# Linear attention and a gated MLP on one core: keys turned to token rows on the array's quarters, odd heads' values stored once, new loads and a new order

## The chip, the cores and the metric

The kernel runs on one core of one Trainium2 chip. The metric is device time in microseconds (us) of one execution. The engines of the core are named as the profile names them: PE (TensorE, matmuls; PEld is its weight load), DVE (VectorE), ACT (ScalarE), POOL (GpSimd) and SP (SyncE), which here only issues DMAs.

## The reference

```python
f = 1.0 / (1.0 + np.exp(-f_logit))                       # (4, 8, 768, 48) each: batch, head, token, dim
for t in range(S):
    state = f[:, :, t, :, None] * state + np.einsum('bhd,bhe->bhde', k[:, :, t], v[:, :, t])
    y[:, :, t] = np.einsum('bhd,bhde->bhe', q[:, :, t], state)
x = y.transpose(0, 2, 1, 3).reshape(B, S, 384)
h = np.maximum(x @ w_in, 0.0)                            # w_in 384 x 1024
u, v = h[..., :512], h[..., 512:]
v_n = (v - mean(v)) / np.sqrt(var(v) + 1e-06)
v_s = np.einsum('ts,bsd->btd', w_spatial, v_n) + b_spatial[None, :, None]
return (u * v_s) @ w_out                                 # w_out 512 x 384
```

The first half is gated linear attention with a forget gate per key dimension. The second half is an MLP in which one half of the hidden layer is mixed over tokens by `w_spatial` and gates the other half.

## The kernel before, in words

The whole kernel is one list of steps, `PLAN`, written out in the file. A step such as `K:4` calls `step_K(4)`, which issues its few instructions at once; every engine then works through its own instructions in that order, and semaphores hold an instruction back until its inputs are there. So the list sets each engine's queue, SP's queue of loads included.

The attention works on 24 chunks n of 128 tokens (4 batch rows of 6 chunks), all 8 heads together. Heads go in pairs: the even head of a pair lies on partitions 0 to 47, the odd one on 64 to 111, and four pairs j lie side by side. The steps of a chunk are:

- `LF`, `LK`, `LQ`: loads of the gate's logits, of keys and queries (tile `fkq`), and of values (`val`). From chunk 8 on `LF` brings logits, keys and queries together.
- `c`, `e`, `z`: the log of the gate and its running sum (chunks 0 to 7 by 8 matmuls with a triangle, L309; later ones by a DVE scan). `h`, `g`, `k`, `q`, `fm`: the decays (`F`), and keys and queries scaled by them.
- `X`: 16 matmuls of 48 by 64, keys against queries within 64 tokens (L359, tile `bp`); `m` masks them on DVE into `sc` (L362).
- `K`: four transposes of 112 by 128 that bring the keys to one token per partition (L341, tile `mm`); `w` copies them to `W` on ACT (L344).
- `kv`: 16 matmuls, keys by values, one sum per 64 tokens (L376, tile `bp`); `r0` and `r1` add them to the state on DVE (`sB`, `sA`).
- `YS`: 16 matmuls, scores by values (L402, `bp`). `Yq`: up to 16, queries by state (L415), added in the same place. `ys` copies the sum to `ysb` on ACT, `xt` transposes it in three pieces (L427), `xh` and `xl` split it into two parts for exact products.

The MLP's steps on PE are `V` (9 matmuls, the half that is normalised, L460), `U` (9, the other half, L545), `S` (18, the spatial mixing, L559) and `O` (12, the output, L590). `vr`, `bs`, `vn`, `vh`, `vl` and others around them normalise on DVE and ACT. `ca`, `ct`, `ch`, `cl` and `wh`, `wl` turn loaded weights into pairs of parts. One `S` needs the normalised rows `vnh`, `vnl` of all six chunks of a batch row.

PSUM is held as four tiles of one bank (`mm`) and two of two banks (`bp`). `take` and `done` hand them out in the order of the list: `X`, `kv` and `Yq`/`YS` each take a `bp` tile, while `K`, `z`, `xt`, `V`, `U`, `S` and `O` take an `mm` tile. A tile is free again when its readers are through.

PE can run as one array of 128 by 128 (here: `K`, `xt`, `V`, `U`, `S`, `O`), as two of 128 by 64 (`z`) or as four quarters of 64 by 64 (`X`, `kv`, `YS`, `Yq`), which work beside each other.

In the code that follows, `even`, `odd`, `low` and `high` are the partition slices 0:48, 64:112, 0:64 and 64:128. Each program line has the number that the profile gives it.

Of the kernel before, what the change touches and what calls it, by code (L numbers as in the profile page):

```python
# [19 lines left out]
T = 128  # L20
# [6 lines left out]
VW = HD + J * D  # L27
# [18 lines left out]
    LF:0 LK:0 constants W0 LF:1 c:0 LQ:1 e:0 LQ:0 z:0 LF:2 c:1 LV:0 e:1 h:0 z:1 g:0 q:0 LK:1 h:1 k:0 g:1 c:2 LW:0,0  # L46
    K:0 fm:0 e:2 fm:1 X:0 LO:1 m:0 ca:V,0 z:2 q:1 w:0 YS:0 k:1 wh:0,0 LK:2 kv:0 ct:V,0 K:1 LQ:2 w:1 ca:O,1 LV:1 r0:0
    ch:V,0 r1:0 Yq:0 ys:0 cl:V,0 X:1 LF:3 h:2 xt:0 LK:3 m:1 g:2 fm:2 q:2 xh:0 YS:1 LW:2,0 ca:V,1 k:2 kv:1 c:3 K:2
    LU:1 ct:V,1 e:3 w:2 z:3 wh:2,0 LQ:3 r0:1 ch:V,1 LB r1:1 Yq:1 cl:V,1 h:3 X:2 LF:4 g:3 LK:4 m:2 fm:3 ca:U,1 q:3
    YS:2 ys:1 LU:0 k:3 kv:2 c:4 xt:1 r0:2 e:4 K:3 xl:0 Yq:2 LQ:4 r1:2 w:3 V:0,0 ys:2 wl:0,0 LK:5 xh:1 wl:2,0 ca:U,0  # L50
    LF:5 xt:2 xl:1 LW:1,0 X:3 vr:0,0 ct:U,0 z:4 xh:2 W1 V:0,1 h:4 g:4 m:3 fm:4 ch:U,0 k:4 YS:3 wh:1,0 xl:2 kv:3
    vr:0,1 K:4 c:5 LQ:5 r0:3 V:0,2 r1:3 e:5 cl:U,0 w:4 q:4 Yq:3 vr:0,2 z:5 ct:O,1 LK:6 ys:3 X:4 h:5 LF:6 U:0,0,1 g:5
    fm:5 nm:0,0 ch:O,1 m:4 U:0,0,0 q:5 vc:0,2 c:6 vc:0,1 k:5 e:6 YS:4 wl:1,0 kv:4 sq:0,1 K:5 ct:U,1 LQ:6 z:6 sq:0,2
    w:5 xt:3 vc:0,0 r0:4 xh:3 r1:4 Yq:4 ch:U,1 xl:3 X:5 LF:7 h:6 cl:U,1 moe V:0,3 LK:7 ys:4 m:5 fm:6 g:6 sq:0,0 q:6
    xt:4 k:6 ur:0,0,1 YS:5 xh:4 na:0,0 kv:5 c:7 nb:0,0 K:6 xl:4 LQ:7 e:7 nc:0,0 U:0,0,2 r0:5 vh:0,0 r1:5 cl:O,1 Yq:5
    vh:0,2 X:6 LO:0 vl:0,0 ur:0,0,2 ys:5 z:7 m:6 vr:0,3 vl:0,2 w:6 YS:6 LF:8 bs:0,3 h:7 kv:6 g:7 xt:5 q:7 V:0,4
    vh:0,1 r0:6 fm:7 LQ:8 r1:6 xh:5 ca:O,0 k:7 Yq:6 xl:5 ur:0,0,0 X:7 LF:9 c:8 vr:0,4 V:0,5 m:7 ys:6 bs:0,4 e:8
# [722 lines left out]
```

## Time and profile before

| what | value |
|---|---|
| median of 3 runs | 370.69 us (369.97 to 371.74) |
| the profiled execution | 371.09 us, of which the span from first to last instruction is 368.9 us |
| PE busy | 349.8 us, 95% of the span |
| DVE, ACT, POOL busy | 219.5, 179.2, 49.7 us |
| mean granted PE clock | 0.974 |
| loaded and stored | 36.27 MB |

A busy PE is one with a matmul under way. Since PE is busy for nearly all of the span, the time is read as PE's work in order of time, plus what it waits for at the start, plus the end after its last matmul.

### The profile page before, as it was taken

The numbers are of one execution on the slowest core, as the hardware profiler recorded it, in microseconds if no ns is written. First come the engines' busy times: TensorE is split into PE (matmuls) and PEld (weight loads), VectorE is DVE, ScalarE is ACT, GpSimd is POOL, SyncE is SP. The second block draws the span as 40 slices with busy tenths as digits, with TensorE's granted clock in tenths as the row PEclk, the third lists the DMA queues.
The fourth block names the chain that finished last, engine by engine and source line by source line (L and its number), as shares of the span: only waits on it lengthen the run. The fifth ranks groups of instructions, "written<-read, shape, count | busy, mean of one in ns | idle before, by whom it ended". The sixth has DMA issues, their size and how long they took to land.

```text
span 368.9 us, 10624 instructions
## 1 busy us (share of the span) xinstructions
PE 349.8 (95%) x4674; PEld 321.0 (87%) x4674; DVE 219.5 (60%) x428; ACT 179.2 (49%) x351; POOL 49.7 (13%) x68
## 2 busy tenths in 40 slices
PE   4589999999999999999999999999999999999992
PEld 3478778889989989999999888999988989999992
DVE  2777788899888555774235898641558537123120
ACT  5774688773574355653135664522355335221121
POOL 3000000001211201012102221032200001122120
PEclk9955999999999999999999999999999999999998
DMA  8997146441554014440045421300171000100102
GB/s 277 351 314 247 49 120 230 121 137 44 151 153 120 0 35 130 123 126 2 0 128 157 140 77 32 118 25 1 34 226 36 2 24 21 44 0 2 43 21 73
DMA packets 13829, 36.27 MB, mean 98 GB/s; under 512 B 1488, under 2 KB 7120, under 8 KB 13776
## 3 DMA queue, kind: packets, MB, share of 16 engines
q1 hardware_dynamic: 13776, 35.53, 31.3%
q8 instruction: 38, 0.62, 0.7%
q14 instruction: 15, 0.12, 0.1%
HBM read 30.80 MB, written 4.72 MB: 96 GB/s over the span
## 4 chain that ended last, share of the span: by engine, by line
PE 86%; DMA 7%; DVE 3%; ACT 1%; SPq 1%; issue 0%; ACTq 0%; DVEq 0%
PE mm L559 28%; PE mm L590 13%; PE mm L460 13%; PE mm L545 13%; DMA fkq<-fkq 4%; PE bp L415 3%; PE bp L402 3%; PE bp L359 3%; DMA fkq<-fn 3%; PE bp L376 3%; PE mm L341 3%; PE mm L427 2%; PE mm L309 1%; DMA out<-osb 1%; DVE fkq L326 0%; SPq L280 0%
## 5 line engine op out<-in xcount | busy, mean ns | idle before, releaser
L575 POOL TENSOR_TENSOR uT<-gt,uT 128x384 f32<-128x384 f32 x32 | 37.7, 1177 | 177.1 <-DVE gt L568 106.9
L583 DVE TENSOR_TENSOR gl<-uT,gh 128x384 fp32r<-128x384 f32 x32 | 18.5, 579 | 40.0 <-ACT gh L579 34.3
L559 PE MATMUL mm<-w_sph,vnh 128*128 128x384 f32 x192 | 40.0, 343 | 0.0
L559 PE MATMUL mm<-w_spl,vnh 128*128 128x384 f32 x192 | 39.0, 338 | 0.0
L559 PE MATMUL mm<-w_sph,vnl 128*128 128x384 f32 x192 | 39.0, 338 | 0.0
L559 PEld LDWEIGHTS mm<-w_sph,vnl 128*128 128x128 f32 x192 | 34.2, 188 | 0.0
L559 PEld LDWEIGHTS mm<-w_spl,vnh 128*128 128x128 f32 x192 | 34.2, 188 | 0.0
L559 PEld LDWEIGHTS mm<-w_sph,vnh 128*128 128x128 f32 x192 | 33.5, 188 | 0.3
L550 ACT ACTIVATE uT<-mm 128x384 f32<-128x384 f32 x32 | 15.7, 490 | 36.7 <-PE mm L545 36.7
L568 DVE TENSOR_TENSOR gt<-mm,b_bc 128x384 f32<-128x384 f32 x32 | 17.7, 553 | 25.8 <-PE mm L559 25.6
L579 ACT CAST gh<-uT 128x384 fp32r<-128x384 f32 x32 | 16.4, 512 | 29.1 <-POOL uT L575 28.2
L336 POOL COPY ends<-F 112x4 f32<-112x4 f32 x24 | 10.1, 425 | 129.2 <-ACT F L315 129.2
L607 ACT COPY osb<-mm 128x384 f32<-128x384 f32 x24 | 11.5, 478 | 32.0 <-PE mm L590 27.0
L545 PE MATMUL mm<-xTh,w_inh 128*128 128x384 f32 x96 | 23.6, 354 | 0.0
L298 ACT ACTIVATE fkq<-fkq 112x512 f32<-112x512 f32 (+1 forms) x24 | 14.3, 596 | 17.4 <-DVE fkq L294 17.3
L460 PE MATMUL mm<-w_inh,xTh 128*128 128x512 f32 x72 | 22.6, 423 | 0.1
L474 ACT ACTIVATE vr<-mm 128x512 f32<-128x512 f32 x24 | 14.3, 596 | 16.7 <-PE mm L460 13.0
L362 DVE TENSOR_TENSOR sc<-bp,mask 128x512 f32<-128x512 f32 x24 | 16.5, 686 | 9.7 <-PE bp L359 9.6
L590 PE MATMUL mm<-w_outh,gh 128*128 128x384 f32 x96 | 22.2, 348 | 0.0
L545 PE MATMUL mm<-xTh,w_inl 128*128 128x384 f32 x96 | 22.1, 338 | 0.0
L545 PE MATMUL mm<-xTl,w_inh 128*128 128x384 f32 x96 | 22.0, 338 | 0.0
L304 DVE TENSOR_TENSOR_SCAN fkq<-runs,fkq 112x512 f32<-112x512 f32 x16 | 19.4, 1217 | 3.4 <-ACT fkq L299 3.3
(102 smaller groups left out, 728.7 us busy)
## 6 DMA issues: line engine op xcount, KB each, us to landing
fkq<-fkq SPq DMA_DIRECT2D x16, 672.0 KB, 4.8
val<-vv SPq DMA_DIRECT2D x24, 288.0 KB, 3.5
out<-osb SPq DMA_DIRECT2D x24, 192.0 KB, 2.2
fkq<-fkq SPq DMA_DIRECT2D x8, 448.0 KB, 4.1
words<-w_cv SPq DMA_DIRECT2D x4, 768.0 KB, 6.7
fkq<-fn SPq DMA_DIRECT2D x8, 192.0 KB, 4.0
late<-w_cv SPq DMA_DIRECT2D x2, 768.0 KB, 7.3
spat<-w_spT SPq DMA_DIRECT2D x3, 384.0 KB, 5.6
```

What stands on the lines that cost most here:

```text
L298: nc.scalar.activation(f, f, AF.Exp, scale=-1.0)
L304: return nc.vector.tensor_tensor_scan(f[0:DP], runs, f[0:DP], 0.0, op0=ALU.mult, op1=ALU.add)
L362: nc.vector.tensor_tensor(Ss[n % 2].rearrange("p (e j t) -> p e j t", e=2, t=C), bp.of(("X", n))[:, :, 0:J * C].rearrange("p e (j t) -> p ...
L460: nc.tensor.matmul(acc, xs[:, c, ut * P:(ut + 1) * P], ws[:, c, G:FF], start=i == 0, stop=i == 3 * KX - 1)
L545: nc.tensor.matmul(acc[:, 0:TH], ws[:, kx, cs], xs[:, kx, :], start=i == 0, stop=i == 3 * KX - 1)
L550: nc.scalar.activation(uTs.take((b, th, c)), mm.of(("u", b, th, c))[:, 0:TH], AF.Relu)
L559: nc.tensor.matmul(acc[:, 0:TH], vns.of((b, ks))[va][:, cs], w_sp_s[wb][:, ks, th * TH:(th + 1) * TH], start=i == 0, stop=i == 3 * KS - 1,)
L568: nc.vector.tensor_tensor(gts.take((b, th, c)), mm.of(("s", b, th, c))[:, 0:TH], b_bc[:, th * TH:(th + 1) * TH], op=ALU.add)
L575: nc.gpsimd.tensor_tensor(uT, gts.of((b, th, c)), uT, op=ALU.mult)
L579: nc.scalar.copy(gs.take((b, th, c), HU)[0], uTs.of((b, th, c)))
L583: nc.vector.tensor_tensor(lo, uTs.of((b, th, c)), hi.bitcast(F32), op=ALU.subtract)
L590: nc.tensor.matmul(acc[:, 0:DM], gs.of((b, th, c))[ga][:, ts], w_out_s[wb][:, c, :], start=c == cs[0] == 0 and ga == wb == 0, stop=c == cs ...
```

## The change

Four things change together.

1. `K` no longer makes four transposes of the whole array. It makes 16 small products against the identity, on the quarters, into the unused columns of the same two banks that hold the chunk's scores. Those that land on partitions 0 to 63 are transposes, those that land on 64 to 127 are ordinary matmuls. `w` then copies 384 columns instead of 448, and `K` takes no `mm` tile. The `bp` tile of the scores is held until both `m` and `w` are through.
2. `kv` writes into the free columns of the bank pair that `YS` has opened, so it follows `YS` and takes no `bp` tile of its own; that pair is held until both `ys` and `r1` are through. Its weights are 48 columns for every head, where the even heads' were 64.
3. Values of odd heads are stored once, with the two halves of the chunk exchanged, instead of twice: a `val` load is 128 x 384 instead of 128 x 576. `fkq` and `w_cv` are laid out in DRAM so that a partition's row comes in three, two or two pieces instead of one. There are four `fkq` tiles instead of three and three `val` tiles instead of two.
4. `PLAN` is a new order of the same 1,079 steps; `W0` and `W1`, which held one `mm` tile for a time and issued nothing, are gone. `LO:1`, `LW:0,0` and others move later, `LF:1` and `LF:3` earlier.

The core of the diff, with the first line of each list:

```diff
-    LF:0 LK:0 constants W0 LF:1 c:0 LQ:1 e:0 LQ:0 z:0 LF:2 c:1 LV:0 e:1 h:0 z:1 g:0 q:0 LK:1 h:1 k:0 g:1 c:2 LW:0,0
+    LF:0 constants LF:1 LQ:1 LK:0 c:0 e:0 LK:1 c:1 e:1 z:0 LV:0 z:1 h:0 g:0 q:0 LQ:0 h:1 k:0 LF:3 g:1 q:1 LV:1 X:0
...
-    ins = tiles(attn, "fkq", 3, [P, 3, J * T])
-    vals = tiles(attn, "val", 2, [P, VW])
+    ins = tiles(attn, "fkq", 4, [P, 3, J * T])
+    vals = tiles(attn, "val", 3, [P, HD])
...
-    Ws = tiles(attn, "W", 2, [P, J * DP])
+    Ws = tiles(attn, "W", 2, [P, 2, J * D])
...
-            nc.sync.dma_start(ins[n % 3][0:DP], fkq[b, u])
+            nc.sync.dma_start(ins[n % 4][0:DP], fkq[b, u].rearrange("i p n -> p i n"))
...
-    def step_K(n):
-        tr = mm.take(("kT", n))
-        for j in range(J):
-            nc.tensor.transpose(tr[:, j * DP:(j + 1) * DP], parts(n)[1][:, j * T:(j + 1) * T], ident[0:DP, 0:DP])
-
-    def step_w(n):
-        nc.scalar.copy(Ws[n % 2], mm.of(("kT", n))[:, 0:J * DP])
-        mm.done(("kT", n))
...
+    def quarters(j):
+        a, b = slice(j * T, j * T + C), slice(j * T + C, (j + 1) * T)
+        return (even, low, a), (odd, high, a), (even, high, b), (odd, low, b)
+
+    def scores(n):
+
+        if ("X", n) not in bp.held:
+            bp.take(("X", n), 2)
+        return bp.of(("X", n))
+
+    def step_K(n):
+        tr = scores(n)
+        for j in range(J):
+            cs = slice(J * C + j * D, J * C + (j + 1) * D)
+            for (e, dr), to, at in quarters(j):
+                k = parts(n)[1][dr, at]
+                if to is low:
+                    nc.tensor.transpose(tr[to, e, cs], k, ident[dr, dr])
+                else:
+                    nc.tensor.matmul(tr[to, e, cs], k, ident[dr, dr], start=True, stop=True)
+
+    def step_w(n):
+        nc.scalar.copy(Ws[n % 2], scores(n)[:, :, J * C:J * C + J * D])
+        bp.done(("X", n))
...
-        W, v, pp = Ws[n % 2], vals[n % 2], bp.take(("kv", n))
+
+        W, v, pp = Ws[n % 2], vals[n % 3], bp.of(("y", n))
...
-            for (e, dr), chunk, rows in ((even, 0, low), (odd, 1, high), (odd, 0, low), (even, 1, high)):
-                out, m = (low, slice(j * DP, j * DP + C)) if e == 0 else (dr, slice(j * DP + C, (j + 1) * DP))
+            for (e, dr), chunk, rows in ((even, 0, low), (odd, 0, high), (even, 1, high), (odd, 1, low)):
...
-                nc.tensor.matmul(pp[out, chunk, cs], W[rows, m], v[rows, hd], start=True, stop=True)
+                nc.tensor.matmul(pp[dr, chunk, J * D:][:, cs], W[rows, e, cs], v[rows, hd], start=False, stop=True, skip_group_check=True)
...
-        bp.done(("kv", n))
+        bp.done(("y", n))
...
-        s, v, y = Ss[n % 2], vals[n % 2], bp.take(("y", n))
+        s, v, y = Ss[n % 2], vals[n % 3], bp.take(("y", n), 2)
...
-        "fkq": np.stack([pairs(f_logit, 10.0), pairs(k, 0.0), pairs(q, 0.0)], axis=3),
+        "fkq": np.stack([pairs(f_logit, 10.0), pairs(k, 0.0), pairs(q, 0.0)], axis=2),
...
-        "vv": np.concatenate([vt, odd], axis=-1),
+        "vv": vt.reshape(B, NU, T, HD),
```

Where the new order bears on the time, the rows of the engines' queues stand as follows. The number behind a name is the buffer: `bp_132` and `bp_133` are the two bank pairs, `fkq_112`, `_113`, `_114` (and `_115`) the tiles of logits, keys and queries, `val_115` and so on the values.

SP's queue of loads from its start, before:

```order
L280 DMA fkq_112<-fn 128x384
L286 DMA fkq_112<-fkq 112x1024
L280 DMA fkq_113<-fn 128x384
L290 DMA val_116<-vv 128x576
L290 DMA val_115<-vv 128x576
L280 DMA fkq_114<-fn 128x384
L225 DMA words_155<-w_cv 128x1536
L286 DMA fkq_113<-fkq 112x1024
L259 DMA spat_157<-w_spT 128x2x384
L225 DMA late_159<-w_cv 128x1536
L286 DMA fkq_114<-fkq 112x1024
```

And now:

```order
L282 DMA fkq_112<-fn 128x384
L282 DMA fkq_113<-fn 128x384
L292 DMA val_117<-vv 128x384
L288 DMA fkq_112<-fkq 112x2x512
L288 DMA fkq_113<-fkq 112x2x512
L224 DMA words_157<-w_cv 128x2x768
L292 DMA val_116<-vv 128x384
L282 DMA fkq_115<-fn 128x384
L224 DMA words_158<-w_cv 128x2x768
L282 DMA fkq_114<-fn 128x384
L224 DMA late_161<-w_cv 128x2x768
```

Keys and queries of chunk 1 (`fkq_113<-fkq`) move from eighth to fifth place, ahead of the first weights; the second half of the weights for `V` (`words_158`) and the logits of chunk 3 (`fkq_115`) come into the first eleven, a `spat` tile and chunk 2's keys leave them.

PE's queue around the keys of chunk 8, between `Yq:7` and the first `V` of batch row 1, before:

```order
L415 MATMUL bp_133<-sB_126,fkq_113 64x48 x2
L341 MATMUL mm_129<-ident,fkq_114 128x112 x4
L359 MATMUL bp_132<-fkq_114 64x64 x16
L427 MATMUL mm_130<-ident,ysb 128x128 x3
L460 MATMUL mm_128<-w_inh,xTh_138 128x512 x3
L460 MATMUL mm_128<-w_inl,xTh_138 128x512 x3
```

And now the keys of a chunk (2), between a transpose of `ysb` and the values of that chunk:

```order
L443 MATMUL mm_133<-ident,ysb 128x128 x3
L375 MATMUL bp_135<-fkq_114 64x64 x16
L362 MATMUL bp_135<-ident,fkq_114 64x48
L364 MATMUL bp_135<-ident,fkq_114 64x48 x2
L362 MATMUL bp_135<-ident,fkq_114 64x48 x2
...
L418 MATMUL bp_134<-val_118,sc_119 64x48 x16
L392 MATMUL bp_134<-val_118,W_121 48x48 x16
```

Before, `K` (L341) is a stretch of the whole array between two stretches of the quarters; now it (L362, L364) continues the quarters that `X` (L375) has begun. Counted over the whole program, PE's tiling changes 113 times before and 90 times now.

PE's queue up to the first `S` (`w_sph`), before, with chunk 8's `YS` and `kv` just ahead of it:

```order
L427 MATMUL mm_130<-ident,ysb 128x128 x3
L460 MATMUL mm_128<-w_inh,xTh_138 128x512 x3
...
L460 MATMUL mm_131<-w_inh,xTh_138 128x512 x3
...
L402 MATMUL bp_133<-val_115,sc_117 64x48 x16
...
L559 MATMUL mm_129<-w_sph,vnh_143 128x384
```

And now, with `kv:6` and `K:7` ahead of it:

```order
L561 MATMUL mm_133<-xTh_136,w_inh 128x384 x3
...
L392 MATMUL bp_135<-val_116,W_121 48x48 x16
L362 MATMUL bp_134<-ident,fkq_115 64x48
...
L561 MATMUL mm_132<-xTh_138,w_inh 128x384 x3
...
L575 MATMUL mm_131<-w_sph,vnh_149 128x384
```

What has moved behind the first `S`: `X`, `YS`, `kv` of chunks 7 and 8, `Yq` and `xt` of 6 and 7, `K:8`, and the `V` of two chunks. On DVE, `cl:U,1`, `ct:O,1`, `cl:O,1` and the `m`, `q`, `k`, `r0`, `r1` and `xl` of those chunks have moved with them, while `ct:O,0` has come ahead of it: 78 DVE steps stand ahead of the last `vl` that the first `S` needs, where 91 stood.

More of the change, by code (lines that the diff above doesn't have):

```diff
@@ L224, in step_L @@
     def step_L(kind, i):
-        nc.sync.dma_start(words_for(kind).take((kind, i), 2)[:, 0:2 * WB], w_cv.bitcast(I32)["VUO".index(kind) * 2 + i])
+        nc.sync.dma_start(
+            words_for(kind).take((kind, i), 2)[:, 0:2 * WB].rearrange("p (h n) -> p h n", h=2),
+            w_cv.bitcast(I32)["VUO".index(kind) * 2 + i].rearrange("h p n -> p h n"),
+        )
     def step_ca(kind, i):
@@ L301, in step_z @@
     def step_z(n):
-        f = ins[n % 3][:, 0]
+        f = ins[n % 4][:, 0]
         if n >= SUMMED:
@@ L336, in step_fm @@
         nc.gpsimd.tensor_copy(ends[:, n * J:(n + 1) * J], end(n).rearrange("p j o -> p (j o)"))
-    def step_K(n):
-        tr = mm.take(("kT", n))
-        for j in range(J):
-            nc.tensor.transpose(tr[:, j * DP:(j + 1) * DP], parts(n)[1][:, j * T:(j + 1) * T], ident[0:DP, 0:DP])
-    def step_w(n):
-        nc.scalar.copy(Ws[n % 2], mm.of(("kT", n))[:, 0:J * DP])
-        mm.done(("kT", n))
     even, odd = (0, slice(0, D)), (1, slice(C, DP))
     low, high = slice(0, C), slice(C, P)
+    def quarters(j):
[18 more added lines that the diff above has]
+        bp.done(("X", n))
     def step_X(n):
         f, k, q = parts(n)
-        sc = bp.take(("X", n))
+        sc = scores(n)
         for j in range(J):
-            cs = slice(j * C, (j + 1) * C)
-            a, b = slice(j * T, j * T + C), slice(j * T + C, (j + 1) * T)
-            for (e, dr), to, at in ((even, low, a), (odd, high, a), (even, high, b), (odd, low, b)):
-                nc.tensor.matmul(sc[to, e, cs], k[dr, at], q[dr, at], start=True, stop=True)
+            for (e, dr), to, at in quarters(j):
+                nc.tensor.matmul(sc[to, e, j * C:(j + 1) * C], k[dr, at], q[dr, at], start=True, stop=True)
     def step_m(n):
@@ L389, in step_r1 @@
             s = sA[(n + 1) % 2]
-            nc.vector.tensor_tensor(s, bp.of(("kv", n))[0:DP, 1, 0:J * D], sB[n % 2], op=ALU.add)
+            nc.vector.tensor_tensor(s, bp.of(("y", n))[0:DP, 1, J * D:2 * J * D], sB[n % 2], op=ALU.add)
             s = s.rearrange("p (j e) -> p j e", e=D)
             nc.vector.tensor_tensor(s, s, end(n).broadcast_to([DP, J, D]), op=ALU.mult)
-        bp.done(("kv", n))
+        bp.done(("y", n))
     def step_YS(n):
-        s, v, y = Ss[n % 2], vals[n % 2], bp.take(("y", n))
+        s, v, y = Ss[n % 2], vals[n % 3], bp.take(("y", n), 2)
         for j in range(J):
             cs = slice(j * D, (j + 1) * D)
-            es, os = slice(j * C, (j + 1) * C), slice((J + j) * C, (J + j + 1) * C)
-            ev, ov = slice(2 * j * D, (2 * j + 1) * D), slice(HD + j * D, HD + (j + 1) * D)
-            for e, to, rows, keys, vs in ((0, low, low, es, ev), (1, low, high, os, ov), (0, high, high, es, ev), (1, high, low, os, ov)):
-                nc.tensor.matmul(y[to, e, cs], s[rows, keys], v[rows, vs], start=j == 0, stop=False, skip_group_check=True)
+            keys = [slice((e * J + j) * C, (e * J + j + 1) * C) for e in range(2)]
+            for e, to, rows in ((0, low, low), (1, low, high), (0, high, high), (1, high, low)):
+                hd = slice((2 * j + e) * D, (2 * j + e + 1) * D)
+                nc.tensor.matmul(y[to, e, cs], s[rows, keys[e]], v[rows, hd], start=j == 0, stop=False, skip_group_check=True)
     def step_Yq(n):
```

155 lines of the change are left out of this document (78 added, 77 removed).

## The prediction

> **What bounds the kernel now.** I read the page's busy rows first, then the span cut into four stretches, then the chain of work within a steady stretch, then what stands at the start.
>
> ```profile
> PE 349.8 (95%) x4674; PEld 321.0 (87%) x4674; DVE 219.5 (60%) x428; ACT 179.2 (49%) x351; POOL 49.7 (13%) x68
> PE   4589999999999999999999999999999999999992
> PEclk9955999999999999999999999999999999999998
> ```
>
> PE is the bound: full from the fourth slice to the last but one. Its clock is halved in the third and fourth slice. The stretches are: up to 30 us, from there to the first `S`, from there to the last matmul, and the end.
>
> ```profile
> core 0: us, PE busy (x) PEld busy (x) DVE busy (x) ACT busy (x) POOL busy (x), PEclk, DMA share, GB/s
> 0.00:30.00 30.00, 18.96 (x420) 16.16 (x421) 18.16 (x35) 19.63 (x33) 3.53 (x16) 0.81 0.94 317
> 30.00:80.64 50.64, 49.96 (x967) 41.23 (x965) 42.58 (x86) 37.83 (x78) 1.38 (x5) 0.95 0.48 142
> 80.64:361.90 281.26, 280.91 (x3294) 263.62 (x3290) 158.78 (x308) 121.26 (x240) 44.82 (x47) 1.00 0.23 68
> 361.90:368.90 7.00, 0.00 (x0) 0.00 (x0) 0.00 (x0) 0.48 (x1) 0.00 (x0) 0.83 0.20 66
> ```
>
> PE idles 11.0 us in the first stretch, 0.7 in the second, 0.35 in the third, 7.0 in the last. The first stretch also has a clock of 0.81, and DMA at 0.94 of its capacity. So there are two ways to gain: less PE work anywhere after 30 us, or a shorter start. DVE is busy for 84% of the second stretch, so it stands close behind PE there.
>
> The prices of PE's steps come from the chain in order of time (start, duration, line, matmul records). From two windows, both at full clock:
>
> ```profile
> 57.30 0.61 PE bp L402 x32
> 57.91 0.45 PE bp L376 x27
> 58.37 0.53 PE mm L341 x4
> 58.90 1.60 PE mm L545 x9
> 60.50 0.61 PE bp L415 x32
> 61.12 0.48 PE bp L359 x32
> 61.60 1.02 PE mm L309 x15
> ...
> 63.68 0.48 PE mm L427 x3
> 64.16 2.09 PE mm L460 x9
> ...
> 66.85 0.48 PE bp L359 x29
> 67.33 2.30 PE mm L460 x9
> 69.62 0.38 PE mm L341 x4
> ```
>
> ```profile
> 102.42 0.62 PE bp L359 x32
> 103.04 0.45 PE bp L415 x32
> ```
>
> The same step costs more where it changes the array's tiling. `Yq` (L415) takes 0.61 after `U` and 0.45 after `X`, so the change to quarters costs 0.16. `V` (L460) takes 2.30 after `X` and 2.09 after `xt`, so the change back costs 0.21; `K` (L341) takes 0.53 after `kv` and 0.38 after `V`, 0.15. I take 0.17 for one change of tiling.
>
> **The change part by part.**
>
> *`K` on the quarters.* Removed: 4 transposes, 0.38 us. Added: 16 products with weights of 64 columns, 48 of them streamed, as in `Yq`. Half are transposes: the whole-array ones left one record each (x4 above for 4), the ordinary ones two (x32 for 16). So 8 + 16 = 24 records instead of 32: between 24/32 of 0.48, 0.36, and all of it, 0.48. Each quarter that makes matmuls still has its 8 records, so I stay near the upper end: 0.45. That is +0.07 us per chunk, +1.7 over 24 chunks (bounds −0.5 and +2.4).
>
> *`kv`.* Same 16 matmuls; weights of even heads shrink from 64 to 48 columns.
>
> ```profile
> L376 PEld LDWEIGHTS bp<-val,W 64*64 64x64 f32 x384 | 14.1, 142 | 1.0 <-issue 0.8 <-ACT fkq L320 0.3
> L376 PEld LDWEIGHTS bp<-val,W 64*48 64x48 f32 x384 | 11.3, 127 | 0.0
> ```
>
> One weight load falls from 142 to 127 ns. If loads set the pace, 0.45 falls in proportion to columns (by 0.11 at most); if not, by nothing. I take 0.04 per chunk, −1.0 in all (bounds 0 and −2.7).
>
> *Changes of tiling.* 113 become 90: 23 x 0.17 = −3.9 us (with 0.15 and 0.21 as ends, −3.5 to −4.8). Between them PE's steady work falls by 3.9 + 1.0 − 1.7 = 3.2 us.
>
> *The copies.* `w` shrinks from 448 to 384 columns on ACT, about 0.05 us a chunk; no term, since ACT has 25% to spare from 30 to 80.64 us and more later. The wait added is that `bp` tiles stay taken until `w` and `r1` as well; what queues behind it on PE is the next `X`/`K` or `YS`. I cost it at 1 us in all (an allowance, less than the 1.05 us that PE idles after 30 us now); it is hidden by the `V`, `U` or `S` between most `X` and the `YS` that needs their tile. Without that cover see the second rival.
>
> *Loads.* Values lose 96 KB per chunk. Rows of `fkq` and `w_cv` come in 2 and 3 KB pieces. The nearest rows for small pieces:
>
> ```profile
> val<-vv SPq DMA_DIRECT2D x24, 288.0 KB, 3.5
> fkq<-fkq SPq DMA_DIRECT2D x8, 448.0 KB, 4.1
> late<-w_spT SPq DMA_DIRECT2D x3, 384.0 KB, 3.8
> ```
>
> 384 KB in pieces of 1.5 KB land in 3.8 us, 448 KB in pieces of 4 KB in 4.1: the same rate, so I cost the layout at nothing. It is covered after 80 us by a DMA share of 0.23. At the start there is no cover: 10% fewer GB/s would delay the first 30 us' data by 3 us.
>
> *The start.* These are the DMA waits on the chain, the first `V`, one of DVE's waits, and a `z` (L309) at half clock:
>
> ```profile
> 4.10 8.03 DMA fkq<-fkq
> 14.01 6.74 DMA fkq<-fn
> 22.29 1.97 PE mm L309 x15
> 31.80 3.99 PE mm L460 x9
> ```
>
> ```profile
> 80.64 1.32 PE L559 MATMUL mm<-w_sph,vnh 128*128 128x384 f32 x6
> ```
>
> The first wait is for chunk 1's keys and queries, issued eighth, landed at 12.13 us behind 2,816 KB. Now they close 1,472 KB, so at the 317 GB/s of the first stretch they land about 4.3 us sooner. The second is for chunk 3's logits, which needed the tile of chunk 0 and were issued at 14.01; with a fourth tile they are eighth in the queue and wait for nothing. Both of the chain's long DMA waits in the start shrink.
>
> What that brings I read at the first `S`, which begins at 80.64 us. With unchanged waits it would begin earlier simply because less stands ahead of it. Moved behind it: two `V` (2 x 2.09), two each of `X`, `YS`, `kv`, `Yq`, `xt` (2 x (0.48 + 0.45 + 0.45 + 0.45 + 0.48)), one `K` (0.38): 9.2 us. The changes of tiling ahead of it fall from 45 to 30: 2.6 us. Eight costlier `K` and seven cheaper `kv`: +0.6 − 0.3. So 80.64 − 9.2 − 2.6 + 0.3 = 69.1 us with the old waits.
>
> Of PE's 11 idle us and the half clock I take 3 back: 66.1 us. The bounds come from DVE, which must feed that `S`. It had done 18.16 + 42.58 = 60.7 us by 80.64, in 91 steps; now 78 steps stand ahead, some 52.1 us (60.7 x 78/91). Never waiting after its first 3 us it would be through at 55; at the pace of before (18.16 by 30 us, then 84%) at 30 + 33.9/0.84 = 70.4. With 20 us done by 30 and 90% after that, 65.7. A pace near 100% is not seen in this trace over such a stretch, so the lower end is 62 (20 by 30, then all of it).
>
> *After the first `S`.* 281.26 us now; plus the 9.2 moved behind it; plus 16 costlier `K` (1.1); minus 17 cheaper `kv` (0.7); minus 8 changes of tiling (1.4): 289.5, and 1 us for new waits: 290.5. The end after the last matmul stays 7.0: the last output tiles are made and stored in the same way.
>
> Sum: 66.1 + 290.5 + 7.0 = 363.6 us of span, 5.3 less than 368.9. The profiled execution took 371.09, 0.4 above the median of 370.69, so on the median 365.4.
>
> *A rule that speaks against it.* `K`'s new transposes run in the column-tiled array, and `xt` and the old `K` ran in the whole one, followed by `V` and `U` at no extra charge (0.38 and 2.09 above); no run here shows an fp32 transpose in a quarter. The Trainium skill, "TensorEngine Tiling (Array Packing)", Restrictions under Tile-to-Partition Mapping, says that column tiling rules out the transpose mode for fp32 on this chip. If the chip ran them as plain products, `K` would be 32 records, 0.48 us, and the sum 364.3 of span instead of 363.6; if it left the tiling for them, that is the fourth rival.
>
> **The rivals.**
>
> First, DVE keeps its pace of before, so that the first `S` comes at 70.4: 70.4 + 290.5 + 7.0 = 367.9 of span. With 1 to 3 us more of waits for data, as PE sits at half clock longer among small steps (15 us of them stand ahead of the first `V` now, 12 before), it is 369 to 371: about no change, 370.5 to 372.5 on the median. For it speak the 0.81 clock and DVE's 84%; against it the loads that come sooner.
>
> Second, it gets slower: bank pairs are released too late. `YS` and `X` wait for `m` and `w`, `ys` and `r1` of the chunk before.
>
> ```profile
> L362 DVE TENSOR_TENSOR sc<-bp,mask 128x512 f32<-128x512 f32 x24 | 16.5, 686 | 9.7 <-PE bp L359 9.6
> ```
>
> One uncovered `m` costs 0.69 us. From 9 uncovered ones on, 6.2 us, the gain with its allowance is gone; at all 24, 16.5 us, the time is 370.69 − 6.3 + 16.5 = 381. Against it: after the first `S`, the lists have a `V`, `U`, `S` or `O` of 1.6 us or more between nearly every such pair; for it: in the first chunks they haven't.
>
> Third, the start gains more: DVE never waits after 30 us, `S` at 62, new `K` at its lower end 0.36 and `kv` at its own: 363.6 − 4.1 − 2.2 − 1.7 = 355.6 of span at the utmost, some 359 if half of that comes.
>
> Fourth, transposes leave the tiling: each `K` changes between transposes and matmuls 8 times. At 0.17 a change that is 1.4 us a chunk, 33 us over 24: 402 on the median. The rows above, where transposes and matmuls follow each other without a charge in the whole array, speak against it.
>
> Fifth, smaller pieces load slower at the start: +3 us, 368.4.
>
> **How the numbers follow.** My forecast (361 to 368.8) has 0.57, the first rival 0.17, the second 0.10, the third 0.10, the fourth 0.03, the fifth 0.03. A measurement of this kernel can tell about 0.5%, 1.9 us, from no change: below 368.8 is faster, above 372.5 slower. Faster are the forecast, the third and most of the fifth: 0.69. No change is most of the first: 0.17. Slower are the second, the fourth and some of the first: 0.14. The range reaches from the third's half, 360, to the first's end, 372.
>
> **What would show it.** First `S` between 62 and 70 us; PE idle in the first 30 us below 9; `K` (both lines together) 0.36 to 0.48 on the chain and `kv` 0.36 to 0.45; 290 us from the first `S` to the last matmul with PE idle under 1.5 there; no long DMA piece on the chain at 14 us. Wrong would be: `m`, `w` or `r1` named as PE's releasers again and again after 80 us; DVE above 95% before the first `S` with PE idle; `K` above 0.6.

## The result, and the profile after

The changed kernel is slower.

| | before | after |
|---|---|---|
| median | 371.22 us (4 runs, 369.97 to 372.45) | 405.22 us (4 runs, 403.48 to 407.58) |
| ratio, with its 95% interval | 1 | 1.092 (1.0846 to 1.0995) |
| the profiled execution, its span | 371.09, 368.9 us | 404.12, 402.4 us |
| first `S`, last matmul's end | 80.64, 361.90 us | 82.65, 395.38 us |

The page's busy rows and the row of PE's clock, after:

```profile
PE 383.5 (95%) x5154; PEld 343.9 (85%) x5154; DVE 218.7 (54%) x428; ACT 176.4 (44%) x351; POOL 48.4 (12%) x68
PEclk9685899999999999999999998999999999999998
```

PE's share of the span is the same 95%, so the time has gone into PE's work: 383.5 us where it was 349.8. The chain of work that ended last, summed by line, names the lines:

```profile
PE 90%; DMA 3%; ACT 3%; DVE 1%; issue 0%; ACTq 0%; DVEq 0%
PE mm L575 26%; PE mm L476 13%; PE mm L561 13%; PE mm L606 12%; PE bp L364 6%; PE bp L362 5%; PE bp L375 4%; PE bp L431 3%; PE bp L418 3%; PE bp L392 2%; DMA words<-w_cv 2%; PE mm L443 2%; PE mm L311 1%; DMA out<-osb 1%; DMA fkq<-fn 1%; ACT fkq L301 1%
```

L364 and L362 are `K`. Together they hold 11% of the chain, where the old `K` (L341) held 3%. One `K` of a steady stretch, in order of time (start, duration, line, records), between an `X` and an `xt`:

```profile
93.52 0.62 PE bp L375 x32
94.15 0.16 PE bp L362
94.31 0.25 PE bp L364 x4
94.56 0.17 PE bp L362 x2
94.72 0.25 PE bp L364 x4
94.97 0.16 PE bp L362 x2
95.13 0.25 PE bp L364 x4
95.38 0.17 PE bp L362 x2
95.55 0.25 PE bp L364 x4
95.79 0.16 PE bp L362
95.95 0.48 PE mm L443 x3
```

`K` begins at 94.15 and the next step at 95.95: 1.80 us, where 0.45 was forecast. It comes in nine groups, transposes (L362) and plain matmuls (L364) in turn, and the length of a group of transposes hardly depends on their number: one takes 0.16, two take 0.17.

The same stretches as in the table of before (start, first `S`, last matmul):

```profile
core 0: us, PE busy (x) PEld busy (x) DVE busy (x) ACT busy (x) POOL busy (x), PEclk, DMA share, GB/s
0.00:30.00 30.00, 22.26 (x430) 18.16 (x430) 17.73 (x34) 17.77 (x31) 3.94 (x16) 0.83 0.88 268
30.00:82.65 52.65, 48.75 (x847) 39.30 (x848) 34.58 (x72) 32.41 (x68) 1.86 (x4) 0.87 0.45 127
82.65:395.38 312.73, 312.50 (x3879) 286.46 (x3877) 166.41 (x325) 125.76 (x251) 42.56 (x48) 0.99 0.20 60
395.38:402.40 7.02, 0.00 (x1) 0.00 (x0) 0.00 (x0) 0.48 (x1) 0.00 (x0) 0.74 0.19 65
```

Against the forecast the first `S` is 16.6 us late (82.65, not 66.1) and the stretch from it to the last matmul 22.2 us too long (312.7, not 290.5); the end is as forecast (7.0). So there are two misses, and the experiments take them in turn. `K` has a part in both: eight `K` stand ahead of the first `S`, sixteen behind it. Ahead of the first `S` PE is busy for 71.0 us and idle for 11.6; before it was 68.9 and 11.7, though less work stands there now.

### The profile page after: what moved, and what is told of

Same layout as the page of the kernel before. It is cut to its first block, busy times and chain, and to the rows that moved or that the text cites. A ratio compares the mean times of both kernels' runs of the same rounds, so it can differ in the third digit from the quotient of the medians.

```text
span 402.4 us, 11593 instructions
## 1 busy us (share of the span) xinstructions
PE 383.5 (95%) x5154; PEld 343.9 (85%) x5154; DVE 218.7 (54%) x428; ACT 176.4 (44%) x351; POOL 48.4 (12%) x68
## 4 chain that ended last, share of the span: by engine, by line
PE 90%; DMA 3%; ACT 3%; DVE 1%; issue 0%; ACTq 0%; DVEq 0%
PE mm L575 26%; PE mm L476 13%; PE mm L561 13%; PE mm L606 12%; PE bp L364 6%; PE bp L362 5%; PE bp L375 4%; PE bp L431 3%; PE bp L418 3%; PE bp L392 2%; DMA words<-w_cv 2%; PE mm L443 2%; PE mm L311 1%; DMA out<-osb 1%; DMA fkq<-fn 1%; ACT fkq L301 1%
## 5 line engine op out<-in xcount | busy, mean ns | idle before, releaser
L591 POOL TENSOR_TENSOR uT<-gt,uT 128x384 f32<-128x384 f32 x32 | 35.6, 1112 | 144.0 <-DVE gt L584 111.8
L599 DVE TENSOR_TENSOR gl<-uT,gh 128x384 fp32r<-128x384 f32 x32 | 18.4, 577 | 40.5 <-ACT gh L595 34.1
L595 ACT CAST gh<-uT 128x384 fp32r<-128x384 f32 x32 | 16.3, 513 | 40.8 <-POOL uT L591 39.3
L367 ACT COPY W<-bp 128x384 f32<-128x384 f32 x24 | 11.5, 479 | 47.3 <-PE bp L362 20.0
L364 PE MATMUL bp<-ident,fkq 48*64 48x48 f32 x384 | 31.3, 241 | 0.0
L362 PE MATMUL bp<-ident,fkq 48*64 48x48 f32 x192 | 28.1, 232 | 0.0
L364 PEld LDWEIGHTS bp<-ident,fkq 48*64 48x64 f32 x384 | 19.2, 135 | 5.4
```

The lines of the kernel that those rows point to most:

```text
L362: nc.tensor.transpose(tr[to, e, cs], k, ident[dr, dr])
L364: nc.tensor.matmul(tr[to, e, cs], k, ident[dr, dr], start=True, stop=True)
L591: nc.gpsimd.tensor_tensor(uT, gts.of((b, th, c)), uT, op=ALU.mult)
L595: nc.scalar.copy(gs.take((b, th, c), HU)[0], uTs.of((b, th, c)))
L599: nc.vector.tensor_tensor(lo, uTs.of((b, th, c)), hi.bitcast(F32), op=ALU.subtract)
```

## The experiments: the price of K

Theory A: inside the quarters, each change between transposes and plain matmuls makes PE run empty. Theory B: the products with the identity are slow in themselves. Theory C: their place in the bank pair or their order among the neighbours costs the time. Four kernels changed `K` alone. All 16 as plain matmuls (`k_allmm`):

```diff
-                if to is low:
-                    nc.tensor.transpose(tr[to, e, cs], k, ident[dr, dr])
-                else:
-                    nc.tensor.matmul(tr[to, e, cs], k, ident[dr, dr], start=True, stop=True)
+                nc.tensor.matmul(tr[to, e, cs], k, ident[dr, dr], start=True, stop=True)
```

> The new kernel with all 16 products of K as ordinary matmuls: no transpose in a quarter is left, so K has no change between transposes and matmuls. Theory A (each such change drains the array, 9 groups of 0.165 or 0.25 us make K's 1.83 us): K falls to about 0.48 us, 24 x 1.35 = 32 us come back, near 373 us, within 1% of the kernel before. Theory B (a product against the identity is slow in a quarter by itself, 0.125 us for a matmul as a quarter of 0.25 for two): K becomes 16 x 0.125 = 2.0 us, 409 us. Theory C (K is not what costs; the new order and the bank pairs held longer do): less than 8 us come back, 397 or more.

All eight transposes first, then the eight matmuls (`k_sorted`; two loops over `quarters(j)` instead of one):

> The new kernel with K's 8 transposes first and its 8 matmuls behind them: the same 16 instructions, one change inside K instead of 8. Theory A: one group of 8 transposes (0.16 and 7 more records of 0.015, about 0.27) and one of 16 matmul records (0.25 and 12 x 0.015, about 0.43): K 0.7 us, 24 x 1.13 = 27 us come back, 378 us. Theory B (the products are slow by themselves): K stays at 1.8 us and the time at 405. Theory C: 405 as well, with K shorter and the time lost elsewhere.

Four transposes, four matmuls, and again (`k_twice`):

> The new kernel with K in two halves, each 4 transposes and then 4 matmuls: 3 changes inside K. Theory A: two groups of 4 transposes (0.21 each) and two of 8 matmul records (0.31 each): K 1.04 us, 386 us, on a line with the 8 changes of the new kernel and the one of the sorted form. Theory B: K 1.8 us, 405 us.

And four transposes of the whole array, as before the change, but into the scores' bank pair (`k_whole`). In this kernel the odd heads' keys stay in the order of the tokens while their stored values are exchanged, so its `kv` sums the odd heads' keys with the values of the other half of the chunk; its work on the chip is otherwise the same.

```diff
-            for (e, dr), to, at in quarters(j):
...
+            cs = slice(J * C + (j % 2) * DP, J * C + (j % 2 + 1) * DP)
+            nc.tensor.transpose(tr[:, j // 2, cs], parts(n)[1][:, j * T:(j + 1) * T], ident[0:DP, 0:DP])
```

> The new kernel with K's four transposes of the whole array as before, but into the scores' bank pair (w copies 448 columns again, kv's weights stay 48 columns). The tiling changes 113 times again instead of 90. Theory A: K 0.38 us, against the form with matmuls alone 24 x 0.10 = 2.4 us less and 23 x 0.17 = 3.9 more, so 1.5 us above that one, about 374.5 us. Theory B: the same K price, but the matmul form is far slower, so this is the faster of the two by 30 us. Theory C: near 400.

| kernel | changes inside `K` | `K` on the chain | median | ratio to before |
|---|---|---|---|---|
| as changed | 8 | 1.80 us | 405.22 | 1.092 (1.0846 to 1.0995) |
| `k_twice` | 3 | 1.13 us | 390.77 (one run) | |
| `k_sorted` | 1 | 0.89 us | 384.90 | 1.0353 (1.0319 to 1.0388) |
| `k_allmm` | 0 | 0.45 us | 377.61 | 1.0151 (1.0116 to 1.0186) |
| `k_whole` | leaves the quarters | 0.39 or 0.53 us | 371.96 | 1.0037 (1.0005 to 1.0068) |

`K` of a steady stretch on the chains, of `k_twice`, `k_sorted` and `k_allmm` in this order (the transposes' line first, the matmuls' line second):

```profile
92.31 0.20 PE bp L366 x4
92.52 0.36 PE bp L368 x8
92.88 0.21 PE bp L366 x4
93.09 0.36 PE bp L368 x8
```

```profile
91.60 0.29 PE bp L365 x8
91.89 0.60 PE bp L367 x16
```

```profile
88.80 0.45 PE bp L361 x32
```

With the same 16 products, `K` takes 0.89, 1.13 and 1.80 us for 1, 3 and 8 changes: 0.12 to 0.13 us for each further change ((1.13 − 0.89)/2 and (1.80 − 1.13)/5). As to the price, Theory A holds; whether PE runs empty at a change, no run shows. Theory B falls with `k_allmm`, where the products with the identity take 0.45 us as plain matmuls, and the transposes are not slow in themselves either: eight in a row take 0.29. Nor is it the going to and fro between the two halves of the columns, since `k_allmm` keeps that order and takes 0.45 all the same. That 0.45 is also the forecast's figure is partly luck: it was meant for 24 records, and for 32 the forecast had 0.48. Theory C would have left 397 us or more there. `k_whole` came 2.5 us under its expectation and `k_allmm` 4.6 over; 3.6 us of stops without a wait, to which the last section returns, stand on the chain of the one ahead of its first `S` and not on that of the other.

A part that A did not say shows too: `k_sorted` takes 0.89 and not the 0.7 expected, and its eight matmuls 0.60. Eight records more take 0.24 us there (0.60 against 0.36 in `k_twice`), while all 32 of `k_allmm` take 0.45, so they run at about half the pace. All of them go to the same half of the columns, so only two of the four quarters work for them, while `k_allmm` keeps four going; this fits the half pace, but no run tests it by itself. In time `k_sorted` came 6.9 us above its expectation and `k_twice`, in its one run, 4.8; their longer `K` makes 4.6 and 2.2 us of it (24 x 0.19 and 24 x 0.09).

The price accounts for the difference: 16 `K` behind the first `S` at 1.80 − 0.45 make 21.6 us, and the stretch is 312.7 in the changed kernel and 291.2 in `k_allmm`, 21.5 apart. The fit is closer than its parts: PE's busy time there is 23.5 us apart (312.5 and 289.0), and `k_allmm` idles for 2.3 us where the changed kernel idles for 0.2. Ahead of the first `S` eight of them make 10.8 us, of which 5.4 show (82.65 against 77.25): PE's busy time falls by 11.9 us, from 71.0 to 59.1, and its idle time grows by 6.5, from 11.6 to 18.1.

The Trainium skill, "TensorEngine Tiling (Array Packing)", Key Properties, says that changing the tiling mode drains the array. Changes of tiling do cost time here, 0.15 to 0.21 us in the rows of before, and so does each change of kind within the quarters, 0.12 to 0.13 us; whether PE leaves the tiling for a transpose or stops for another reason, no run shows.

## The experiments: the start

With `K` at the forecast price, `k_allmm` is still 1.5% slower than before. Its rows up to the first `S` and from there to the last matmul:

```profile
0.00:30.00 30.00, 17.02 (x454) 14.36 (x454) 16.79 (x32) 16.60 (x29) 3.49 (x16) 0.88 0.89 267
30.00:77.25 47.25, 42.11 (x887) 35.30 (x887) 35.58 (x72) 33.59 (x71) 1.79 (x4) 0.86 0.46 134
77.25:368.46 291.21, 288.96 (x4007) 271.42 (x4006) 165.07 (x325) 125.63 (x251) 42.70 (x48) 1.00 0.23 66
```

From the first `S` on it takes 291.2 us (290.5 forecast). All the rest is the start. The first `S` comes sooner than before, at 77.25, but by the forecast's count 9.2 us of work have moved behind it: it should have come at 66.1. PE is idle for 18.1 us ahead of it (before: 11.7), and the loads of the first 30 us come at 267 GB/s (before: 317). What it waits for on the chain from 3 us, and SP's issues at the same time (line, tensors, how many; of a row of two, the first duration includes the wait between them):

```profile
3.18 8.45 DMA words<-w_cv
11.65 0.95 ACT words L233
12.61 0.38 ACT W L364
...
14.06 2.17 issue
...
24.50 7.99 DMA words<-w_cv
32.52 0.89 ACT words L233
33.41 0.37 ACT W L364
33.83 0.89 PE bp L389 x32
```

```profile
19.59 4.32 SPq L292 DMA_DIRECT2D val<-vv  x2
23.96 0.43 SPq L261 DMA_DIRECT2D spat<-w_spT  x1
24.50 0.40 SPq L224 DMA_DIRECT2D words<-w_cv  x1
```

The conversions `ca:V,0` and `ca:U,0` (L233) wait on ACT for weights, and `w` (L364) stands behind them in ACT's queue; `kv` (L389) waits for `w`. The weights of the second came late because SP, which issues in order, stood at the value load `LQ:4` until `kv:1` had freed a tile. These waits go by the order of the list; the rate need not. The row of 2.17 us of `issue` is a stop without a wait, to which the last section returns. The first four runs separated layout and order. The diffs of the list show only the piece that changes.

`old_layout`, which is `k_allmm` with `fkq` and `w_cv` laid out as before (one piece a row):

> The kernel with all 16 key products as plain matmuls, and with keys, queries, logits and weights laid out in DRAM as before: a partition's row in one piece of 6 KB (or 4 KB) instead of two or three. The order of the steps is the new one. Theory L (the smaller pieces move slower: from 4 to 8 us the DMA engines were busy for 0.94 and moved 255 GB/s, before 1.04 and 360): DMA back at 320 GB/s or more over the first 30 us, the half words load in 6.5 to 7 us instead of 8.2, first S at 71 to 73 us instead of 77.25, time 372 to 374. Theory O (the new order makes loads wait in SP's queue, the layout is innocent): rates as with the pieces once DMA is busy, first S at 76 to 77, time 376 to 378.

`before_pieces`, the kernel before with the new layout only:

> The kernel before, with nothing changed but the layout in DRAM: fkq in three pieces of 2 KB and w_cv in two of 3 KB. Theory L: the loads in the first 30 us fall from 317 to about 275 GB/s, first S moves from 80.64 to 84 to 86 us, time 374 to 377. Theory O: first S within 1 us of 80.6, time within 1 us of the kernel before.

`early_w`:

```diff
-k:1 ca:V,0 K:0 m:0 fm:1 X:1 fm:0 w:0 K:1 ct:V,0 LF:2 YS:0 w:1 LO:0
+k:1 K:0 m:0 fm:1 X:1 fm:0 w:0 K:1 LF:2 YS:0 w:1 ca:V,0 ct:V,0 LO:0
```

> The kernel with all 16 key products as plain matmuls, and with ca:V,0 and ct:V,0 (which wait for the first weights, landed at 11.6 us) moved behind w:0 and w:1 in the list, so that ACT copies the first chunk's keys at once. There w:0 stood behind ca:V,0 on ACT, kv:0 behind w:0, and the third value load in SP's queue waited for kv:0 until 16.65 us with all later loads behind it. Theory O: that load is issued at 11 to 13 us, DMA's gap at 13 to 16.6 us closes, first S 3 to 4 us sooner (73 to 74), time 373 to 375. Theory L: DMA is slow rather than late; first S at 76 to 77, time 376 to 377.5.

`start3`, the edits of `old_layout` and `early_w` together on `k_allmm`, and

```diff
-kv:0 ca:V,1 r0:0 LQ:3 ch:V,0 r1:0 Yq:0 LK:3
+kv:0 ca:V,1 r0:0 LK:3 LK:2 LQ:2 LQ:3 ch:V,0 r1:0 Yq:0
```

> All of it together: plain matmuls for the keys, the layout of before, ca:V,0 and ct:V,0 behind w:1, and the three loads that wait for no tile (LK:3, LK:2, LQ:2) ahead of the value load LQ:3 that does. If both theories hold in part, first S at 67 to 70 us and time 367 to 370, faster than the kernel before by 0.3 to 1%. Theory L alone: as with the old layout (372 to 374). Theory O alone: as with the earlier w (373 to 375). If the first S stays at 76 or later, the start is bound by something else (the half clock, or DVE).

| kernel | first `S` | first 30 us | median | ratio to before |
|---|---|---|---|---|
| `k_allmm` | 77.2 us | 267 GB/s | 377.61 | 1.0151 (1.0116 to 1.0186) |
| `old_layout` | 76.4 | 271 | 377.61 | 1.0199 (1.0157 to 1.0240) |
| `before_pieces` | 83.9 (before: 80.6) | 280 (before: 317) | 373.38 | 1.0031 (0.9995 to 1.0067) |
| `early_w` | 76.1 | 259 | 376.90 | 1.0172 (1.0133 to 1.0211) |
| `start3` | 79.0 | 260 | 378.84 | 1.0189 (1.0138 to 1.0240) |

Theory L holds for the old order at most in part: in its one profile the rate falls from 317 to 280 GB/s and the first `S` comes 3.3 us later, yet the time is not told from the kernel before. In the new order the old layout brings back neither rate nor time, so L isn't the cause there. Theory O falls as it was put: to take one wait out of the queue of loads gains 1.1 us at the first `S` and nothing in the time. `start3` gained nothing either: the logits, with keys put ahead of them, now stood on its chain for 7.65 and 7.97 us. Two kernels of this table have the same median and ratios of 1.0151 and 1.0199, so ratios less than half a per cent apart don't tell kernels from each other here.

The next four tried PE's own order and the weights. In `early_v` the first two `V` move ahead of steps that wait:

```diff
-xt:1 wh:1,0 k:2 q:3
+xt:1 V:0,0 wh:1,0 k:2 q:3
...
-YS:2 kv:2 c:5 LU:1 X:3 xl:1 e:5
+YS:2 kv:2 vr:0,0 xl:1 V:0,1 c:5 LU:1 X:3 e:5
```

> All 16 key products as plain matmuls; in the list the first V (V:0,0) stands behind xt:1 and the second (V:0,1) behind kv:2, ahead of the steps of chunks 2 and 3 and of c:5, instead of behind them; nothing else moves. Theory P (PE is idle from 28 to 34 us because its next step waits for w:2, which stands on ACT behind the conversion ca:U,0 of weights issued at 24.5 us, and on DVE xl:1 stands behind c:5 whose logits land as late): the first V begins at 25 to 28 us instead of 41, PE's idle time up to 60 us falls by 3 to 4 us, first S at 73 to 74, time 373 to 375. Theory Q (the start is bound by what the loads bring, 8.0 MB by 30 us instead of 9.5, whatever waits for it): PE idles later instead, first S at 76 to 77, time 376 to 378.

In `lazy`, that and `LO:0`, `ca:O,0`, `wh:1,0`, `wl:1,0`, `wh:0,0`, `ca:U,0` and `LW:0,0` behind the first two `V`; it also has the edit of `early_w`, and `LF:5` ahead of `LU:0`:

> As early_v, and the work on weights that nothing before the first V needs moves behind it: the load and conversion of the output weights (LO:0, ca:O,0), the conversions wh:1,0, wl:1,0, wh:0,0 and ca:U,0, the load LW:0,0; ca:V,0 and ct:V,0 stand behind w:1, and LF:5 ahead of LU:0. Theory P: no load that is needed waits behind 768 KB that isn't, first S at 69 to 72, time 369 to 372. Theory Q: what moves must be loaded all the same before the first S (except 768 KB, 2.4 us at 317 GB/s): first S at 74 to 76, time 374 to 377.

`whole`, a `K` as in `k_whole`, with `w` in three copies so that odd heads' keys and values meet:

```diff
...
+        nc.scalar.copy(W[:, 0], tr[:, :, :, 0:D])
+        nc.scalar.copy(W[low, 1], tr[high, :, :, C:DP])
+        nc.scalar.copy(W[high, 1], tr[low, :, :, C:DP])
```

> The changed kernel with K as four transposes of the whole array into the scores' bank pair; three copies instead of one bring the odd heads' keys to the half of the partitions where their values lie. Everything else as changed. If only K's price differs from the kernel with 16 plain matmuls (0.39 to 0.53 us instead of 0.45, two changes of tiling a chunk more, but no time in which PE waits for nothing that the profile shows): first S at 73 to 74, time 371 to 373, within 0.5% of the kernel before. If the two more copies on ACT matter at the start: first S at 75 to 76, time 374 to 375.

`whole_lazy`, `whole` with the list of `lazy`:

> The whole-array K with three copies, and the list of the kernel lazy. Theory P: first S at 66 to 69 us, time 364 to 368, faster than the kernel before by 1 to 2%. Theory Q: first S at 71 to 73, time 369 to 372, no difference that can be told.

| kernel | first `S` | median | ratio to before |
|---|---|---|---|
| `early_v` | 77.3 us | 376.16 | 1.0124 (1.0058 to 1.0189) |
| `lazy` | 81.5 | 378.32 | 1.0175 (1.0109 to 1.0240) |
| `whole` | 74.7 | 374.38 | 1.0081 (1.0043 to 1.0119) |
| `whole_lazy` | 76.9 | 379.25 | 1.0231 (1.0177 to 1.0285) |

Both `lazy` kernels missed on the wrong side of every theory. Their traces show a wait of their own: `LW:0,0` now waited in SP's queue for `w_spl`, 8.0 us in `lazy` and 10.5 in `whole_lazy`, and `wh:0,0` on ACT for that load. `early_v` filled the gap with a `V` and met the next wait at once: `ca:U,0` still waited until 32.7 us, with `w:2` behind it. So one hold after another covers the same stretch. `whole` has its first `S` 1.5 us later than `k_whole` (73.2), so the two more copies on ACT may cost something there, but the times of single executions of one kernel differ by as much. The next four took the two that are left singly, and together with the early `V`. `u_late`:

```diff
-LW:2,0 ca:U,0 m:2 fm:3 LW:0,0 w:2
+LW:2,0 m:2 fm:3 LW:0,0 w:2
...
-Yq:2 w:3 z:5
+Yq:2 w:3 ca:U,0 z:5
```

> All 16 key products as plain matmuls, and one step moved: ca:U,0, which waits on ACT for weights that land at 32.5 us, stands behind w:3 instead of ahead of w:2. Theory R (ACT's queue behind ca:U,0 is what PE waits for): w:2 copies at 27 to 30 us instead of 33.4, PE's idle 3.15 us from 30 to 40 us fall below 1, first S at 74 to 75, time 374 to 375. Theory T (the chunks' own chain, logits and keys that land late, would hold PE at the same place): first S at 76 to 77.5, time 376 to 378.

`sp_free`:

```diff
-h:2 LQ:2 LQ:4 g:2 xl:0
+h:2 LQ:2 g:2 xl:0
...
-X:2 LF:5 K:2
+X:2 LF:5 LQ:4 K:2
```

> All 16 key products as plain matmuls, and one load moved: the value load LQ:4, which waits in SP's queue for kv:1 until 24 us with LW:1,0, LU:0, LK:5 and LF:5 behind it, stands behind LF:5. Theory R' (that wait is what makes the loads late): LU:0 is issued at 19 to 21 us and lands at 27 to 29, first S at 74 to 75, time 374 to 375. Theory T: DMA is at its full share from 20 to 30 us anyway, what is issued sooner takes from LK:4 and LK:2; first S within 1 us of 77.25, time 376 to 378.

`both_v`, these two and `early_v`; `whole_both_v`, the same list with the `K` of `whole`:

> The two together, and the first two V early as in early_v. Theory R and R': first S at 70 to 73 us, time 370 to 373. Theory T: first S at 75 to 77, time 375 to 378.

> The list of both_v with K as four transposes of the whole array and three copies of the keys. Theory R and R': first S at 68 to 71 us, time 366 to 370, between no difference from the kernel before and 1% faster. Theory T: first S at 73 to 75, time 372 to 375.

| kernel | first `S` | median | ratio to before |
|---|---|---|---|
| `u_late` | 77.5 us | 377.20 | 1.0174 (1.0123 to 1.0225) |
| `sp_free` | 78.6 | 379.94 | 1.0248 (1.0205 to 1.0291) |
| `both_v` | 71.0 | 372.38 | 1.0065 (1.0030 to 1.0100) |
| `whole_both_v` | 73.5 | 373.88 | 1.0104 (1.0063 to 1.0144) |

Alone, none of the three edits brings anything (77.3, 77.5, 78.6), and `sp_free` is slower than `k_allmm` by intervals that don't overlap; so alone they come closest to Theory T, or Q. Together they bring 6.2 us at the first `S`, as R had it. The windows of `k_allmm` and then of `both_v` show where the two part:

```profile
20.00:28.00 8.00, 6.64 (x152) 5.47 (x151) 6.49 (x12) 5.97 (x12) 0.97 (x2) 0.81 1.03 268
28.00:34.00 6.00, 2.39 (x104) 2.10 (x108) 2.66 (x4) 2.95 (x5) 0.00 (x0) 0.65 1.05 308
34.00:40.00 6.00, 5.58 (x148) 5.00 (x144) 4.73 (x9) 4.56 (x8) 0.94 (x1) 0.50 0.60 214
```

```profile
20.00:28.00 8.00, 7.92 (x155) 6.73 (x155) 6.39 (x11) 5.95 (x12) 0.46 (x2) 0.85 1.01 282
28.00:34.00 6.00, 5.19 (x163) 4.00 (x165) 3.52 (x7) 2.59 (x7) 0.00 (x0) 1.00 1.05 301
34.00:40.00 6.00, 3.72 (x148) 3.15 (x143) 4.82 (x9) 5.46 (x10) 0.19 (x1) 1.00 0.63 216
```

In `k_allmm` PE works for 2.39 of the 6 us from 28 to 34, and then at half the clock; in `both_v` for 5.19, at a whole clock there and in the next window, where a stop of 2.28 us holds it to 3.72. The DMA share from 28 to 34 is the same, 1.05, so the loads seem to set the gap only through the queues that stand behind them. Over the whole way to the first `S`, shorter waits are the smaller part of the gain: on the same 1,341 records PE's idle time falls from 18.1 to 16.3 us and its busy time from 59.13 to 54.75. The mean granted clock there is 0.87 and 0.95, but `early_v`, with 0.93, is busy for 60.5, so that the clock makes the busy time shorter is not shown. With the whole-array `K` the same list brought 1.2 us at the first `S` (74.7 to 73.5) and no better time (1.0081 and 1.0104, with overlapping intervals), where Theory R had 366 to 370: its fit with `both_v` does not carry over.

The last two went on from `both_v`: `best` adds the layout of before and the edit of `early_w`; `best_lo` moves `LO:0` behind `LQ:6` and `ca:O,0` ahead of `ct:O,0` as well.

> The kernel both_v with the layout of before in DRAM and with ca:V,0 and ct:V,0 behind w:1. Theory U (each late thing adds once nothing else hides it): those two brought 0.8 and 1.1 us alone, together 2 to 4 now; first S at 67 to 69 us, time 368.5 to 371, no difference from the kernel before. Theory V (PE's stops without a wait, 4.6 us of the chain before the first S in both_v, and the half clock are what is left): first S at 70 to 71, time 371 to 373.

> The kernel best, and the load of half the output weights (LO:0, 768 KB, 2.4 us of DMA at 317 GB/s) and its conversion ca:O,0 moved behind the first V. Theory U: 1 to 2.4 us more, first S at 65 to 67.5, time 367 to 370. Theory V: first S within 1 us of best, time within 1 us.

`best` has its first `S` at 72.4 us and takes 373.34, ratio 1.0048 (1.0015 to 1.0081); `best_lo` 70.5 us and 372.73, 1.0035 (1.0004 to 1.0067). Theory U falls. V is nearer, though `best` lies a little above its bounds (71 us and 373). None of the versions beats the kernel before; the best ones come to within 0.5% of it. In `best` the clock is 1.00 all through the start, against 0.81 in the first 30 us of the kernel before, so a whole clock there is not enough to gain.

What V names stands on the chain of `both_v`:

```profile
13.27 0.35 PE bp L389 x29
13.62 2.26 issue
15.88 0.41 PE bp L389 x3
...
34.75 0.12 PE bp L428 x4
34.87 2.28 issue
37.15 0.69 PE bp L428 x28
```

PE stops twice in the middle of a step, 4.5 us together, and waits for nothing that the profile shows. That is close to the 4.9 us by which `both_v` misses the forecast's 66.1, but it does not prove that the first `S` would come there without them: `whole_both_v` has the same list and no such stop above 0.3 us on its chain up to there, and its first `S` comes at 73.5.

## Why the prediction was wrong, point by point

- **`K` on the quarters, 0.45 us: the step that failed.** The forecast counted records (24 instead of 32, kept at 0.45) and took it that transposes and matmuls follow each other in the quarters as freely as in the whole array. The rows behind that, `K` then `V`, were of the whole array only. Measured: 1.80, so `K` costs 24 x 1.42 = 34.1 us more than the old one, where 1.7 was counted. The fourth rival, at 0.03, had a charge for each of the 8 changes, which is what the runs show, but its size holds by luck. It took 0.17 a change where 0.12 to 0.13 are measured, and the rest of the 1.80 is matmuls at half the pace. And its 33 us on top of the forecast's 365.4 would be 398, not 402; the start, which missed too, makes up for it in the measured 405.2. The rule of the Trainium skill that the prediction itself cites was a reason to give it more than 0.03, since no row of the trace spoke for transposes in quarters either.
- **First `S` at 66.1: the second step that failed.** The forecast's count, put on PE's busy time, leaves 57.4 us of work ahead of it (68.9 − 9.2 − 2.6 + 0.3), and it takes 3 us back "of PE's 11 idle us and the half clock". In the changed kernel these 3 us did not come: PE idles for 11.6 us, as before (11.7), and its clock from 30 us to the first `S` is 0.87 where it was 0.95. The other 13.6 us are work, 71.0 instead of 57.4, of which eight `K` make 10.8. With `K` at its forecast price the first `S` still came only at 77.25: the work was then about as counted (59.1), but PE idled for 18.1 us, 3.6 of them in stops without a wait. The forecast looked at two loads that come sooner, and not at what stands ahead of `w:0`, `w:2` and `xl:1` on ACT, DVE and SP in the new list. Taking away three holds brought 6.2 us of the 11.15 back, most of it as shorter busy time; two unexplained stops of PE stand in the rest with 4.5. What else holds the first `S` back stays open.
- **From the first `S` to the last matmul, 290.5: right, once `K` is priced right.** `k_allmm` takes 291.2. That it fits so well is partly luck: 1.7 us in it are two stops without a wait, which nobody forecast, and the forecast has 1 us for new waits that did not come. Fewer changes of tiling and cheaper `kv` (0.36 us on the chain, near the lower bound of its term; 0.41 was taken) are in it. The end, 7.0, is right.
- **New waits, 1 us: none.** After the first `S` PE's waits in the changed kernel are one row, so the second rival (bank pairs released too late) is refuted:

```profile
PE mm L443 <- ACT ysb L434: 0.2, 1, 0.2
```

- **DVE's pace, the first rival:** not it. Up to the first `S` DVE is busy for 34.58 of 52.65 us after 30; it waits with the others.
- **Smaller pieces, the fifth rival, +3 us:** in the old order the profile's first `S` moved by 3.3 us, but the time's ratio is 1.0031 (0.9995 to 1.0067), not told from no change; in the new order the old layout brought nothing.

## What to carry to other kernels

Before an operation is moved into another mode of the array, ask which row shows it in that mode; if none does, price each change of kind as a stop, and count the changes within the step, not only around it. Where a start is full of in-order queues, taking one wait away may bring nothing and three together something (here 6 us at the first `S`, of which 1.9 are shorter waits): read on each queue what stands ahead of the step that PE waits for, and count the loads that those steps need.

## What the runs showed of the hardware

- In quarters, fp32 transposes against the identity leave one record each and run, but each change to or from plain matmuls costs 0.12 to 0.13 us; 16 plain matmuls against the identity take 0.45 us in all behind another step of the quarters.
- PE stops of 1 to 2.8 us without a visible wait came in every kernel with 16 plain matmuls for `K`, the first of them in several at the same matmul (after 29 of 32 records of a `kv`). They do not appear on the chain of the changed kernel, which has nearly as many PE records (5,154 against 5,346) but takes longer over them. The kernels with the whole-array `K` have none above 0.6 us, `k_twice` none above 0.91 and `k_sorted` none above 1.05. Of the 30 such stops on the chains of the kernels with 16 plain matmuls, 29 begin behind 1 us in which DMA is at 0.96 of its share or more. One, 1.96 us at 38.08 us of `start3`, begins behind 0.44 and has 0.05 in it. A supply of instructions that can't follow long runs of short matmuls, above all beside busy DMA, would fit: the DMA queue that the profile calls `instruction` carries 44 packets in `k_allmm`, 42 in the changed kernel and 38 with the whole-array `K`. This is argued, not shown. The window of one stop, in `k_allmm`, with PE idle and DMA at 1.05:

```profile
207.74:209.11 1.37, 0.00 (x1) 0.00 (x2) 0.08 (x1) 0.00 (x0) 0.00 (x0) 1.00 1.05 279
```

- In `k_allmm` a stretch in which PE was busy for 2.39 of 6 us was followed by 6 us at half the clock. A gap in the start can so cost twice; but in `both_v` PE was busy for 3.72 of 6 us at a clock of 1.00, and how long a gap must be, no run shows.
